# A recurrent memory layer's softmax: eight groups on one path, the last four on ScalarE and GpSimd, and a filler unit in three parts

## The chip, the core and the metric

The kernel runs on one core of one Trainium2 chip. A core has five engines that run side by side and meet through semaphores: TensorE (PE in the profile; its weight loads are listed as PEld), VectorE (DVE), ScalarE (ACT), GpSimd (POOL) and SyncE (SP), whose queue issues most DMAs here. The metric is the device time of one execution, in microseconds; lower is better. The kernel before takes 2867.46 us (median of 3 runs, 2866.17 to 2868.26).

## What is computed

Four layers run one after the other, A, B, A, B, each added to the residual stream x (2048 tokens of width 640), each behind a LayerNorm. The change lies in layer B, a transformer with recurrent memory:

```python
def _B_ref(x, mem0, Wq, Wk, Wv, Wo, seg_len):   # H = 32 heads of Dh = 128, M = 8, seg_len = 32
    mask = (idx[:, None] < M) | (idx[:, None] >= idx[None, :])
    mem = mem0
    for s in range(n_seg):                       # 64 segments
        xs = x[:, s * seg_len:(s + 1) * seg_len, :].copy()
        h = jnp.concatenate([mem, xs], axis=1)   # 8 memory rows, then 32 tokens
        q, k, v = (jnp.einsum('btd,dhe->bhte', h, W) for W in (Wq, Wk, Wv))
        scores = jnp.where(mask[None, None], jnp.einsum('bhqe,bhke->bhqk', q, k) * scale, -1e9)
        p = _softmax(scores, axis=-1)
        o = jnp.einsum('bhqk,bhke->bhqe', p, v)
        o = jnp.einsum('bhte,hed->btd', o, Wo)
        mem = o[:, :M, :].copy()                 # the next segment starts from these rows
        outs.append(o[:, M:, :])
```

The memory rows of a segment are the output of the segment before, so the 64 steps of a layer B can't overlap freely: the projections of step s+1 need the output rows of step s.

## The kernel before

`layer_B` (line 543 on) runs its 64 steps in one loop. All instructions are issued through a recording layer (`_OrdEng`, line 91 on; that is why almost all of B's instructions carry line 105 in the profile, and are told apart by their tiles). It chains the instructions of TensorE, ScalarE, VectorE and GpSimd in the order in which the program writes them. So the order in the source is the order in each of these engines' queues, and an instruction that waits holds all that stand behind it on its engine. SyncE's queue isn't chained: a scheduler places the DMAs in it.

A step s works on 32 columns: eight rows of memory for the next segment and 24 tokens of this one. In order:

- *Projections.* `thin_mm` multiplies the 32 columns by four blocks of the weights (b_Ka, b_Qa, b_Kb, b_Qb: 20 matmuls each). The results are copied to SBUF (b_kq), transposed (b_TPak, b_TPaq, b_TPbk, b_TPbq), and scattered to b_KT and b_QT.
- *Scores.* There are 12 groups of 128 rows by 40 keys. Groups 0 to 7 lie in one PSUM tile (b_SP0), groups 8 to 11 in a second (b_SP1); `GR` holds these bounds.
- *Softmax.* `soft_max` takes the negated row maximum of a tile (VectorE), `soft_sub` adds it to the scores in PSUM (VectorE), `soft_exp` takes the exponential into E_ (ScalarE), `soft_sum` sums the rows (VectorE). One reciprocal makes rs for all 12 groups, and `soft_p` multiplies: columns 32 to 40 into Pm, columns 0 to 32 into Px (VectorE).
- *Behind it on GpSimd*, `tails_copy(s + 1)` copies the scores' operands of the next segment's last eight tokens from b_tl to b_QZ and b_KT. b_tl is one buffer, loaded by SyncE (`tails_load`).
- *V.* b_Va and b_Vb, 20 matmuls each, need no softmax; ScalarE copies them to b_Vth.
- *Tail unit.* In the first 55 steps of a layer (s up to 54), `tail_unit` computes eight heads (five matmuls each, b_tail) for the last eight tokens of later segments. The kernel before puts five heads ahead of the transposes of P and three behind them; `tail_evac` then copies the result (b_tu, ScalarE) and stores it. The last nine steps of a layer have no such unit.
- *Transposes of P.* `p_transp(0)` transposes groups 4 to 7 and 0 to 3, `p_transp(1)` groups 8 to 11 and again 0 to 3, first from Pm, then from Px, into b_PTP. They are copied to SBUF: b_PTa by ScalarE in two halves, b_PTb by VectorE.
- *PV and the output.* `pv(0)` reads b_PTa, `pv(1)` b_PTb; both write four tiles b_OTP, which VectorE and ScalarE copy to b_OTsb. Matmuls with b_wo follow (b_OPSd for the rows of four segments together, b_OPS), a copy of the result (b_msb), and the transposes of the memory rows (b_MT), which VectorE writes into the next columns (b_HX). There the next step starts.

Tiles that change hands every step are few: E_, Px, Pm, b_PTa and b_PTb have one buffer each, negmax, ssum and rs two. The tiles of PSUM from `ps_tile` share five buffers, b_tail has one of its own.

Of the kernel before, what the change touches and what calls it, by code (L numbers as in the profile page):

```python
# [18 lines left out]
F32 = mybir.dt.float32  # L19
BF16 = mybir.dt.bfloat16  # L20
ACT = mybir.ActivationFunctionType
ALU = mybir.AluOpType
# [15 lines left out]
def alloc_consts(tc, ctx):  # L38
    cp = ctx.enter_context(tc.tile_pool(name="consts", bufs=1))
    C = Consts()  # L40
    C.pool = cp
    C.identb = cp.tile([128, 128], BF16, name="c_identb")
    C.mhalf = cp.tile([128, 1], F32, name="c_mhalf")
    C.negu = cp.tile([128, 2, 128], BF16, name="c_negu")
    C.krow = cp.tile([128, 1], F32, name="c_krow")
    C.bdmask = cp.tile([128, 128], F32, name="c_bd")
    W = AWeights()
    W.g = cp.tile([128, 32], F32, name="a_g")
    W.omg = cp.tile([128, 32], F32, name="a_omg")
    return C, W  # L50


def build_consts(nc, tc, C):
    with ExitStack() as tctx:
        tp_ = tctx.enter_context(tc.tile_pool(name="consts_tmp", bufs=1))
        ones = tp_.tile([128, 128], F32, name="c_ones")
        nc.vector.memset(ones[:], 1.0)
        identf = tp_.tile([128, 128], F32, name="c_identf")
        nc.gpsimd.affine_select(out=identf[:], in_=ones[:], pattern=[[-1, 128]], compare_op=ALU.is_equal,
                                fill=0.0, base=0, channel_multiplier=1)  # L60
        nc.vector.tensor_copy(C.identb[:], identf[:])
        nc.vector.memset(C.mhalf[:], -0.5)
        negs = tp_.tile([128, 128], F32, name="c_negs")
        nc.vector.memset(negs[:], -1e9)
        neguf = tp_.tile([128, 128], F32, name="c_neguf")
        nc.gpsimd.affine_select(out=neguf[:], in_=negs[:], pattern=[[1, 128]], compare_op=ALU.is_gt,
                                fill=0.0, base=0, channel_multiplier=-1)
        for i in range(2):
            nc.vector.tensor_copy(C.negu[:, i, :], neguf[:])
        krows = tp_.tile([128, 4, 2], F32, name="c_krows")  # L70
        nc.vector.tensor_copy(krows[:], identf[:].rearrange("p (j s) -> p j s", s=32)[:, :, 20:22])
        nc.vector.tensor_reduce(out=C.krow[:], in_=krows[:].rearrange("p j s -> p (j s)"), axis=AX.X, op=ALU.add)
        nc.vector.memset(C.bdmask[:], 0.0)
        for j in range(4):
            nc.vector.memset(C.bdmask[32 * j:32 * j + 32, 32 * j:32 * j + 32], 1.0)
# [467 lines left out]
def layer_B(nc, tc, C, W, x_src, xb_src, x_dst, mem0, B_Wv, B_Wo, nsteps=64, out_bf16=False, tag=""):  # L543
    SCB = 1.0 / math.sqrt(128.0)
    nc_raw = nc
    nc = _OrdNC(tc, nc_raw, engines=ORDER_ENGINES)
# [4 lines left out]
    with ExitStack() as ctx:  # L551
# [21 lines left out]
        def ps_tile(shape, dtype, name):  # L573
            return pp.tile(shape, dtype, name=name, tag="ps")


        Px = st.tile([128, 12, 32], BF16, name="b_Px")
        Pm = st.tile([128, 12, 32], BF16, name="b_Pm")
# [39 lines left out]
        def evac(eng, dst, src, scale=None):  # L618
            if eng == "act":
                if scale is None:  # L620
                    nc.scalar.copy(dst, src)
                else:
                    nc.scalar.activation(out=dst, in_=src, func=ACT.Copy, scale=scale)
            else:
                if scale is None:
                    nc.vector.tensor_copy(dst, src)
                else:
                    nc.vector.tensor_scalar(out=dst, in0=src, scalar1=scale, scalar2=None, op0=ALU.mult)
# [72 lines left out]
        def tail_unit(T, k, i0, i1, shared=False):  # L701
            proj, hg = divmod(k, 4)
            Wt = W.wk if proj else W.wq
            if i0 == 0:
                if shared:
                    tail_ps[0] = ps_tile([128, 8, 64], F32, "b_tail")
                else:
                    tail_ps[0] = po.tile([128, 8, 64], F32, name="b_tail", tag="tail")
            ps = tail_ps[0]
            for i in range(i0, i1):  # L710
                h = 8 * hg + i
                for c in range(NCH):
                    nc.tensor.matmul(ps[:, i, :], lhsT=Wt[:, c, 128 * h:128 * h + 128], rhs=TX[T][:, c, :, :].rearrange("p s t -> p (s t)"),
                                     start=(c == 0), stop=(c == NCH - 1))
# [139 lines left out]
        for s in range(nsteps):  # L854
# [3 lines left out]
            unit = None  # L858
            if (s + 1) // 8 + 1 < NT:
                unit = ((s + 1) // 8 + 1, (s + 1) % 8)  # L860
# [15 lines left out]
            GR = ((0, 8), (8, 12))  # L876

            def mask_mm(a):
                g0, g1 = GR[a]
                SP = ps_tile([128, g1 - g0, 40], F32, f"b_SP{a}")  # L880
                nc.tensor.matmul(SP[:].rearrange("p g k -> p (g k)"), lhsT=C.identb[:], rhs=mask12[:, g0:g1, :].rearrange("p g k -> p (g k)"),
                                 start=True, stop=False, skip_group_check=True)
                return SP
# [18 lines left out]
            negmax = sm.tile([128, 12], F32, name="b_negmax", tag="negmax")  # L902
            ssum = sm.tile([128, 12], F32, name="b_ssum", tag="ssum")
            rs = sm.tile([128, 12], F32, name="b_rs", tag="rs")
            E_ = wk.tile([128, 12, 40], BF16, name="b_E", tag="E0")

            def soft_max(a, SP):
                nc.vector.tensor_reduce(out=negmax[:, slice(*GR[a])], in_=SP[:], axis=AX.X, op=ALU.max, negate=True)

            def soft_sub(a, SP):  # L910
                n_ = GR[a][1] - GR[a][0]
                nc.vector.tensor_tensor(out=SP[:], in0=SP[:], in1=negmax[:, slice(*GR[a])].unsqueeze(2).to_broadcast([128, n_, 40]), op=ALU.add)

            def soft_exp(a, SP):
                nc.scalar.activation(out=E_[:, slice(*GR[a]), :], in_=SP[:], func=ACT.Exp)

            def soft_sum(a):
                nc.vector.tensor_reduce(out=ssum[:, slice(*GR[a])], in_=E_[:, slice(*GR[a]), :], axis=AX.X, op=ALU.add)

            def soft_p(P_, k0, k1, g0, g1):  # L920
                nc.vector.tensor_tensor(out=P_[:, g0:g1, 0:k1 - k0], in0=E_[:, g0:g1, k0:k1],
                                        in1=rs[:, g0:g1].unsqueeze(2).to_broadcast([128, g1 - g0, k1 - k0]), op=ALU.mult)

            def p_transp(b):
                ptp = ps_tile([128, 2, 4, 40], F32, "b_PTP")
                sel = C.identb[:, 64 * b:64 * b + 64].rearrange("p (i c) -> p i c", c=32)[:, :, 0:16]
                for part, P_ in ((1, Pm), (0, Px)):
                    nc.tensor.matmul(ptp[:, part, :, 8:40], lhsT=P_[:, 4 + 4 * b:8 + 4 * b, :].rearrange("p g k -> p (g k)"), rhs=C.identb[:],
                                     start=True, stop=True, skip_group_check=True)
                    nc.tensor.matmul(ptp[:, part, :, 0:8], lhsT=P_[:, 0:4, :].rearrange("p g k -> p (g k)"), rhs=sel,  # L930
                                     start=True, stop=True, skip_group_check=True)
                return ptp
# [33 lines left out]
            SPb = mask_mm(1)  # L966
            scores((SPa, SPb))
            soft_max(0, SPa)
            soft_max(1, SPb)
            soft_sub(0, SPa)  # L970
            soft_exp(0, SPa)
            soft_sub(1, SPb)
            soft_exp(1, SPb)
            soft_sum(0)
            soft_sum(1)
            nc.vector.reciprocal(out=rs[:], in_=ssum[:])
            soft_p(Pm, 32, 40, 0, 12)
            soft_p(Px, 0, 32, 0, 8)
            soft_p(Px, 0, 32, 8, 12)
            if not last:  # L980
                tails_copy(s + 1, tl)
            VH[s] = w2.tile([128, 2, 512], BF16, name="b_Vth", tag="Vth")
# [3 lines left out]
            evac("act", VH[s][:, 1, :], Vb[:])  # L986

            if unit:
                tail_unit(unit[0], unit[1], 0, 5)
            if ln_ready:  # L990
                ln_spread(ln_ready.pop(0))
            ptpa = p_transp(0)
            PTa = wk.tile([128, 2, 4, 40], BF16, name="b_PTa", tag="PTa")
            for hf in range(2):
                evac("act", PTa[:, :, 2 * hf:2 * hf + 2, :], ptpa[:, :, 2 * hf:2 * hf + 2, :])
            ptpb = p_transp(1)
            PTb = wk.tile([128, 2, 4, 40], BF16, name="b_PTb", tag="PTb")
            evac("dve", PTb[:], ptpb[:])
            if unit:
                tail_unit(unit[0], unit[1], 5, 8)  # L1000
                tail_evac(unit[0], unit[1], "act")
            ots = [ps_tile([128, 2, 4, 40], F32, "b_OTP") for _ in range(4)]
            pv(0, PTa, ots)
# [144 lines left out]
```

## Time and profile before

| | |
|---|---|
| median of three runs | 2867.46 us (2866.17 to 2868.26) |
| the profiled execution | 2871.54 us |
| its span, first to last instruction | 2869.8 us |
| mean granted clock of TensorE | 0.975 |
| one step of B with a tail unit, from one b_Ka to the next (most of them) | 14.97 to 15.4 us |
| one step of B without a tail unit | 14.97 us, or about 16.7 us |
| b_ssum, eight groups / four groups (VectorE) | 486 / 309 ns |
| b_SP minus its maximum, eight / four (VectorE) | 490 / 323 ns |
| b_E, eight / four (ScalarE) | 437 / 298 ns |
| b_Px, eight / four (VectorE) | 418 / 284 ns |
| b_PTa, one of two halves (ScalarE) / b_PTb (VectorE) | 300 / 492 ns |

The profile lists each instruction with its engine, its start and its end. A group's row reads: line, engine, operation, output tile from input tile, shapes and types, count, then busy time, mean duration, and the idle time of the engine ahead of it with what ended most of it. A row "x2" in a timeline joins two neighbours of one kind, and its length runs from the start of the first to the end of the last. The chain of waits follows the work back from the last instruction, at each step to what released it. A row of windows gives, for a stretch, the busy time of each engine and the clock that TensorE was granted. TensorE's matmuls are pipelined, and their ends are modelled.

### The profile page before, as it was taken

The numbers are of one execution on the slowest core, as the hardware profiler recorded it, in microseconds if no ns is written. First come the engines' busy times: TensorE is split into PE (matmuls) and PEld (weight loads), VectorE is DVE, ScalarE is ACT, GpSimd is POOL, SyncE is SP. The second block draws the span as 40 slices with busy tenths as digits, with TensorE's granted clock in tenths as the row PEclk, the third lists the DMA queues.
The fourth block names the chain that finished last, engine by engine and source line by source line (L and its number), as shares of the span: only waits on it lengthen the run. The fifth ranks groups of instructions, "written<-read, shape, count | busy, mean of one in ns | idle before, by whom it ended". The sixth has DMA issues, their size and how long they took to land.

```text
span 2869.8 us, 145239 instructions
## 1 busy us (share of the span) xinstructions
PE 2671.2 (93%) x64776; PEld 1669.4 (58%) x64776; DVE 1646.2 (57%) x4428; ACT 1555.7 (54%) x3390; POOL 633.2 (22%) x1506
## 2 busy tenths in 40 slices
PE   5899998999999999999969999889999999999988
PEld 2455555666666666665535555556666666666655
DVE  5778854555555555544468878545555555555544
ACT  3777863545445455544438777544455455445533
POOL 3456551100000000000025666400000000010000
PEclk8999999999999999999989999999999999999999
DMA  5110144222221122111130111621111111111110
GB/s 212 53 43 28 33 142 118 44 43 43 44 43 42 42 46 43 40 40 29 23 120 20 57 47 35 198 71 40 42 39 38 43 41 41 42 39 38 38 22 19
DMA packets 322947, 156.40 MB, mean 54 GB/s; under 512 B 245776, under 2 KB 311056, under 8 KB 319248
## 3 DMA queue, kind: packets, MB, share of 16 engines
q1 hardware_dynamic: 320880, 136.63, 18.8%
q8 instruction: 506, 8.29, 1.2%
q10 hardware_dynamic: 1440, 10.49, 1.0%
q14 instruction: 121, 0.99, 0.1%
HBM read 95.65 MB, written 51.38 MB: 51 GB/s over the span
## 4 chain that ended last, share of the span: by engine, by line
PE 61%; DVE 13%; ACT 4%; DMA 3%; issue 2%; POOL 1%; SPq 0%; ACTq 0%; DVEq 0%; POOLq 0%
PE b_OPS L105 11%; PE b_Ka L105 6%; PE b_Qb L105 5%; PE b_Kb L105 5%; PE b_Qa L105 5%; PE b_SP L105 4%; PE b_OTP L105 3%; PE b_OPSd L105 3%; DVE b_ssum L105 3%; PE b_tail L105 2%; PE b_vtail L105 2%; DVE b_negmax L105 2%; PE b_PTP L105 2%; DVE b_SP L105 2%; ACT b_E L105 2%
## 5 line engine op out<-in xcount | busy, mean ns | idle before, releaser
L105 PEld LDWEIGHTS <-b_HX 128*32 128x32 bf16 x15360 | 412.1, 97 | 374.1 <-issue 16.5
L375 DVE TENSOR_REDUCE a_nm<-a_S 128x2 f32<-128x1024 f32 (+3 forms) x512 | 403.5, 811 | 92.3 <-PE a_T L407 70.8
L410 ACT ACTIVATE a_PT<-a_T 128x1024 bf16<-128x1024 f32 (+1 forms) x384 | 341.0, 892 | 51.9 <-PE a_T L407 46.7
L105 POOL COPY b_OTdef<-b_OTsb 128x256 bf16<-128x256 bf16 x128 | 51.2, 400 | 1360.0 <-DVE b_OTsb L105 1288.6
L105 PE MATMUL b_OPS<-b_wo,b_OTsb 128*32 128x320 bf16 x8192 | 327.0, 311 | 12.7 <-issue 7.6
L105 PEld LDWEIGHTS <-b_OTsb 128*32 128x32 bf16 x8192 | 217.0, 100 | 104.2 <-DVE b_OTsb L105 28.1
L412 POOL TENSOR_SCALAR_AFFINE_SELECT a_PT<-a_PT 128x256 bf16<-128x256 bf16 (+1 forms) x384 | 197.3, 516 | 235.6 <-ACT a_PT L410 234.4
L105 ACT CAST b_msb<-b_OPS 128x128 bf16<-128x128 f32 x252 | 61.5, 295 | 294.2 <-PE b_OPS L105 294.2
L105 DVE CAST b_HX<-b_MT 128x16 bf16<-128x16 f32 x248 | 44.2, 178 | 268.8 <-PE b_MT L105 257.5
L105 ACT CAST b_kq<-b_Kb 128x512 bf16<-128x512 f32 x128 | 74.9, 585 | 201.4 <-PE b_Kb L105 201.4
L105 DVE TENSOR_SCALAR b_kq<-b_Qa 128x512 bf16<-128x512 f32 x128 | 88.5, 692 | 157.3 <-PE b_Qa L105 157.2
L105 DVE CAST b_OTsb<-b_OTP 128x160 bf16<-128x160 f32 (+1 forms) x384 | 122.0, 373 | 90.5 <-PE b_OTP L105 90.4
L105 PE MATMUL b_Ka<-b_wk,b_HX 128*32 128x512 bf16 x2520 | 159.2, 381 | 6.0 <-DVE b_HX L105 0.3
L105 PE MATMUL b_Va<-b_wv,b_HX 128*32 128x512 bf16 x2520 | 161.0, 380 | 0.0
L105 PE MATMUL b_Vb<-b_wv,b_HX 128*32 128x512 bf16 x2520 | 160.3, 379 | 0.0
L407 PE MATMUL a_T<-a_q,a_kT 32*128 32x512 bf16 (+3 forms) x1024 | 139.5, 306 | 21.2 <-DVE a_nm L375 14.6
L105 DVE COPY b_KT<-b_TPak 128x128 bf16<-128x128 bf16 x128 | 28.7, 224 | 227.2 <-PE b_TPak L105 227.2
L105 PE MATMUL b_Qb<-b_wq,b_HX 128*32 128x512 bf16 x2520 | 157.9, 379 | 0.0
L105 PE MATMUL b_Qa<-b_wq,b_HX 128*32 128x512 bf16 x2520 | 157.8, 379 | 0.0
L105 PE MATMUL b_Kb<-b_wk,b_HX 128*32 128x512 bf16 x2520 | 157.8, 379 | 0.0
L105 PEld LDWEIGHTS <-b_kq 128*128 128x128 bf16 x2080 | 116.9, 98 | 69.9 <-ACT b_kq L105 55.6
L105 ACT CAST b_kq<-b_Ka 128x512 bf16<-128x512 f32 x128 | 74.9, 585 | 147.0 <-PE b_Ka L105 147.0
(196 smaller groups left out, 5586.7 us busy)
## 6 DMA issues: line engine op xcount, KB each, us to landing
b_QKd<-b_tu SPq DMA_DIRECT2D x128, 128.0 KB
b_tl<-b_QKd SPq DMA_DIRECT2D x128, 128.0 KB
b_wv<-in_B_Wv_dram SPq DMA_DIRECT2D x10, 1024.0 KB
b_wo<-in_B_Wo_dram SPq DMA_DIRECT2D x16, 640.0 KB
b_VTd<-b_vt SPq DMA_DIRECT2D x256, 32.0 KB
b_Vth<-b_VTd SPq DMA_DIRECT2D x512, 16.0 KB
b_XO<-xres SPq DMA_DIRECT2D x256, 30.0 KB
b_wk<-in_B_Wk_dram ACTq DMA_DIRECT2D x5, 1024.0 KB
```

The costliest lines, as they stand in the source:

```text
L105: r = f(*a, **k)
L375: nc.vector.tensor_reduce(out=nm[:, qc, 2 * pr:2 * pr + 2], in_=X[:, :, o:o + w_], axis=AX.X, op=ALU.max, negate=True)
L407: nc.tensor.matmul(Y[:, e, o:o + w_], lhsT=kT[rows, 128 * kc:128 * kc + 128], rhs=q2[rows, 128 * kc:512], start=True, stop=True, tile_posi ...
L410: nc.scalar.activation(out=PT[:, :, b:b + width], in_=Y[:, :, 0:width], func=ACT.Exp, scale=SC)
L412: nc.gpsimd.affine_select(out=dv, in_=dv, pattern=[[0, 2], [0, diag], [1, 128]], compare_op=ALU.is_ge, fill=0.0, base=0, channel_multiplie ...
```

## The change

- The softmax of groups 0 to 7 runs to its end ahead of the rest: the maximum of the last four groups is taken after the subtraction of the first eight, and the sum, the reciprocal and the products of the first eight follow without the others.
- The last four groups aren't subtracted on VectorE. ScalarE takes their exponential one group at a time, in four instructions, with the negated maximum as a bias per row and the row sum as a second output (`soft_exp_rows`).
- Their reciprocal is taken on GpSimd as a power of minus one (`C.mone` is a new constant of -1), and GpSimd also makes their Pm and Px, ahead of `tails_copy`.
- `p_transp(0)` reads only what VectorE made; `p_transp(1)` waits for GpSimd.
- b_PTa is copied whole, by VectorE; b_PTb by ScalarE.
- The tail unit stands in three parts: four heads ahead of `p_transp(0)`, two between it and `p_transp(1)`, two behind.

In the built program SyncE's queue differs too: the load of b_tl for a later segment stands ahead of the store of b_tu and the loads of b_Vth, where it stood behind them.

```diff
@@ constants @@
+    C.mone = cp.tile([128, 1], F32, name="c_mone")
...
+        nc.vector.memset(C.mone[:], -1.0)
@@ layer_B @@
+            def soft_exp_rows(a, SP):
+                g0, g1 = GR[a]
+                for g in range(g0, g1):
+                    nc.scalar.activation(out=E_[:, g, :], in_=SP[:, g - g0, :], func=ACT.Exp, bias=negmax[:, g:g + 1], scale=1.0,
+                                         accum_out=ssum[:, g:g + 1])
...
-            def soft_p(P_, k0, k1, g0, g1):
-                nc.vector.tensor_tensor(out=P_[:, g0:g1, 0:k1 - k0], in0=E_[:, g0:g1, k0:k1],
-                                        in1=rs[:, g0:g1].unsqueeze(2).to_broadcast([128, g1 - g0, k1 - k0]), op=ALU.mult)
+            def soft_p(eng, P_, k0, k1, g0, g1):
+                eng.tensor_tensor(out=P_[:, g0:g1, 0:k1 - k0], in0=E_[:, g0:g1, k0:k1],
+                                  in1=rs[:, g0:g1].unsqueeze(2).to_broadcast([128, g1 - g0, k1 - k0]), op=ALU.mult)
...
             soft_max(0, SPa)
-            soft_max(1, SPb)
             soft_sub(0, SPa)
             soft_exp(0, SPa)
-            soft_sub(1, SPb)
-            soft_exp(1, SPb)
+            soft_max(1, SPb)
+            soft_exp_rows(1, SPb)
             soft_sum(0)
-            soft_sum(1)
-            nc.vector.reciprocal(out=rs[:], in_=ssum[:])
-            soft_p(Pm, 32, 40, 0, 12)
-            soft_p(Px, 0, 32, 0, 8)
-            soft_p(Px, 0, 32, 8, 12)
+            nc.vector.reciprocal(out=rs[:, 0:8], in_=ssum[:, 0:8])
+            soft_p(nc.vector, Pm, 32, 40, 0, 8)
+            soft_p(nc.vector, Px, 0, 32, 0, 8)
+            nc.gpsimd.tensor_tensor(out=rs[:, 8:12], in0=ssum[:, 8:12], in1=C.mone[:, 0:1].to_broadcast([128, 4]), op=ALU.pow)
+            soft_p(nc.gpsimd, Pm, 32, 40, 8, 12)
+            soft_p(nc.gpsimd, Px, 0, 32, 8, 12)
...
             if unit:
-                tail_unit(unit[0], unit[1], 0, 5)
+                tail_unit(unit[0], unit[1], 0, 4)
...
-            for hf in range(2):
-                evac("act", PTa[:, :, 2 * hf:2 * hf + 2, :], ptpa[:, :, 2 * hf:2 * hf + 2, :])
+            evac("dve", PTa[:], ptpa[:])
+            if unit:
+                tail_unit(unit[0], unit[1], 4, 6)
             ptpb = p_transp(1)
...
-            evac("dve", PTb[:], ptpb[:])
+            evac("act", PTb[:], ptpb[:])
             if unit:
-                tail_unit(unit[0], unit[1], 5, 8)
+                tail_unit(unit[0], unit[1], 6, 8)
                 tail_evac(unit[0], unit[1], "act")
```

## The prediction

> **What bounds the kernel now.** I read the page first, its chain of waits, then that chain in order of time for one step of B, then the windows that show the clock.
>
> ```profile
> PE 2671.2 (93%) x64776; PEld 1669.4 (58%) x64776; DVE 1646.2 (57%) x4428; ACT 1555.7 (54%) x3390; POOL 633.2 (22%) x1506
> PE 61%; DVE 13%; ACT 4%; DMA 3%; issue 2%; POOL 1%; SPq 0%; ACTq 0%; DVEq 0%; POOLq 0%
> ...
> 1154.52 0.55 DVE b_negmax L105 x2
> ...
> 1155.16 0.50 DVE b_SP L105
> ...
> 1155.74 0.45 ACT b_E L105
> ...
> 1156.21 0.72 DVE b_ssum L105 x2
> ...
> 1156.96 0.24 DVE b_rs L105
> ...
> 1157.22 0.26 DVE b_Pm L105
> 1157.48 0.34 DVE b_Px L105
> ...
> 1157.87 0.45 PE b_PTP L105 x6
> 1158.32 0.45 PE b_tail L105 x15
> ```
>
> A busy share of 93% would say that TensorE sets the time. The chain says otherwise: in every step it leaves TensorE for the softmax and returns at the transposes of P, although V and 25 tail matmuls run meanwhile. I call 1154.52 zero of this step. The transposes of the eight groups' Px start at 3.35, those of the last four at 3.45 (Pm) and 3.56 (Px), and the part of PV that reads PTb starts at 4.42 (timeline of TensorE). From there all is one chain to the next step, so what moves 4.42 moves the step, and 128 steps run one after the other. 110 of them hold a tail unit (s up to 54, in two layers); 18 don't.
>
> ```profile
> 1308.70:1312.10 3.40, 2.26 (x92) 1.68 (x88) 2.14 (x9) 1.51 (x5) 0.00 (x0) 1.00 0.07 15
> 1312.10:1315.50 3.40, 3.40 (x56) 2.00 (x56) 1.55 (x5) 0.48 (x2) 1.21 (x4) 0.51 0.10 25
> ...
> 1325.80:1329.20 3.40, 2.33 (x100) 1.80 (x104) 2.32 (x9) 1.69 (x6) 0.00 (x0) 1.00 0.00 0
> 1329.20:1332.60 3.40, 3.40 (x60) 2.10 (x52) 0.27 (x1) 0.09 (x1) 1.22 (x4) 0.50 0.12 28
> 1342.90:1346.30 3.40, 2.80 (x112) 2.17 (x116) 2.21 (x7) 1.33 (x5) 0.06 (x1) 1.00 0.00 0
> 1346.30:1349.70 3.40, 2.92 (x84) 1.71 (x80) 0.99 (x4) 0.49 (x2) 1.16 (x4) 1.00 0.08 20
> ```
>
> The columns are stretch, length, busy time of PE, PEld, DVE, ACT, POOL, then granted clock. These are steps without a tail unit. Where PE was idle 1.14 or 1.07 us of 3.4, the next 3.4 us ran at half clock; after 0.60 idle they didn't. A halved step takes 16.75 us (K projections at 1317.11 and 1333.86), the next, unhalved one 14.97: 1.78 us. 12 of the 18 were halved, none of the 110.
>
> **The change, part by part.** DVE first. It loses the second subtraction (323 ns), the second sum (309), the second Px (284) and a third of Pm. Eight groups in the new order: reduce 0 to 0.49; subtraction 0.52 to 1.01; exp on ScalarE from 1.10 for 0.44, to 1.54; the second reduce lies under it (0.93 to 1.24); sum 1.57 to 2.05; reciprocal to 2.31; Pm 2.35 to 2.60; Px, which overlaps Pm by 0.08, 2.52 to 2.94. Durations are the groups' means, gaps those of the chain. Before, Px was ready at 3.31 (1157.83), so the first half comes 0.37 earlier. TensorE is there in time: 20 tail matmuls at 0.035 (15 took 1158.17 to 1158.70) from 2.13 end at 2.83, the first Px transposes start at 3.00, end their issue at 3.10, and 10 tail matmuls more bring TensorE to the last four groups at 3.45.
>
> Those go ScalarE, GpSimd, TensorE. The rows:
>
> ```profile
> L297 ACT ACTIVATE a_kT<-a_KP,c_krow 128x512 bf16<-128x512 f32 x64 | 44.0, 687 | 27.3 <-PE a_KP L295 27.0
> L105 ACT ACTIVATE b_E<-b_SP 128x160 bf16<-128x160 f32 x128 | 38.2, 298 | 0.0
> L105 POOL TENSOR_TENSOR b_ln_rstd<-b_ln_rstd,c_mhalf 128x1 f32<-128x1 f32 x32 | 17.5, 548 | 370.4 <-DVE b_ln_rstd L105 355.5 <-DMA b_Vth<-b_VTd 14.9
> L380 POOL TENSOR_TENSOR a_NM<-a_nm,a_NM 128x16 bf16<-128x16 f32 x64 | 17.2, 268 | 0.7
> 1566.61 1.09 POOL L86 TENSOR_TENSOR a_ln_rstd<-a_ln_rstd,c_mhalf 128x1 f32<-128x1 f32 x1
> 1566.62 0.68 DVE L286 SCALAR_TENSOR_TENSOR a_phiq<-a_EQ,a_rq 128x512 bf16<-128x512 bf16 x1
> ```
>
> *Four rows of exp with bias and sum.* exp costs 298 ns for 160 columns and 437 for 320, so 40 cost 194; a column operand adds 102 (687 against 585 for the same shape without), neighbours overlap 0.10. First row at 1.44, the end A at the least 1.44 + 0.296 + 3 x 0.196 = 2.32. No row shows the summing output. Its bounds: nothing, or one smallest ScalarE instruction without overlap (229 ns, 128x32) per row, A = 2.32 + 4 x 0.23 = 3.24. I take the middle, 2.8, since a read-out of one column should cost less than 32.
>
> *pow of four columns.* pow of one column is 548 ns, a plain two-input op of 16 columns 268. Bounds: 0.55, if further columns are as cheap as plain ones, and 0.55 + 3 x 0.28 = 1.39. I take 0.85, nearer to the row of the same operation.
>
> *Pm and Px on GpSimd.* 16 columns 268, 128 columns 469, so 32 cost about 0.29; with a gap of 0.08 after pow, which it reads (as L446 behind L445, 3.5 us in 48), and an overlap of 0.06 (b_OTdef 1162.27 for 0.40, the next copy at 1162.61), 0.08 + 0.29 + 0.47 - 0.06 = 0.78. Starting pow after ScalarE is 0.07 (the mask op at L412 after L410), waking TensorE 0.05.
>
> So the last transposes start at R = A + 0.07 + pow + 0.78 + 0.05: **4.55** (2.8, 0.85), from 3.77 (2.32, 0.55) to 5.53 (3.24, 1.39). Below nothing the sum can't go: TensorE is there at 3.45 in any case.
>
> The last lines shown speak against the low end. pow took 1.09 instead of 0.55 beside a DVE op of two SBUF inputs that ran 0.68; it ended 0.40 after that op. For A under 2.8 the new pow lies beside DVE's Pm and Px (to 2.94), and would end at 3.34 at the earliest: R = 4.17. [...]
>
> *What is late next.* PTb's eviction begins 0.34 after the transposes start (1157.87 to 1158.21), takes 0.43 on ScalarE, and TensorE answers in 0.05. So PV's second part starts at R + 0.82 and not at 4.42: R - 3.60 = **0.95 a step**, bounds 0.17 and 1.93, and 128 x 0.95 = 122 us. On ScalarE, V's evictions move behind the rows (end A + 0.97 = 3.8, before PTb needs it at 4.9); PTa goes to DVE, 3.34 to 3.83, under tail matmuls; the tail's eviction follows PTb and ends about when PV does, as now. If that cover goes it adds 0.1. GpSimd's three tail copies (0.3, 0.3, 0.4) now stand behind Px, and the load of b_tl, which waits for them, stands in SP's queue ahead of the stores of b_tu and the loads of b_Vth: at R + 1 = 5.5 against 4.94 for b_tu now (1159.46). Those loads are wanted a step later, 10 us off: nothing. The LayerNorm pow and OTdef follow on GpSimd at about 7: nothing.
>
> *The clock.* TensorE now stands from 3.45 to R, 1.10 us in a unit step, on the edge of the 1.07 that halved it. A free window of 3.41 holds 1.07 of it in (3.41 + 1.10 - 2.14)/3.41 = 0.69 of positions; half of the steps will fall below the edge, so I charge a third: 110 x 0.33 x 1.78 = 65 us. The steps without a unit wait longer: the other 6 are halved too, 11 us.
>
> Sum: 122 + 65 + 11 = 198 us. The profiled execution took 2871.5 (span 2869.8, 1.7 around it), 4.1 over the median of 2867.5, so **3065**. [...]
>
> **The rivals.**
> *GpSimd quick (chance 0.23).* Rows and pow near the low ends: R 3.77 to 4.17, 0.17 to 0.57 a step. TensorE waits at most 0.72, under the edge, so no clock. 22 to 73 us and 11: 2900 to 2951. For it: pow's 548 ns may be mostly its start. Against: it takes both ends at once.
> *The clock in most steps (0.26).* R from 4.8: waits of 1.35 to 2.08, 1.2 to 1.93 a step, halved in 0.77 to 0.98 of unit steps: 154 + 151 + 11 to 247 + 192 + 11: 3184 to 3318. For it: pow costs 548 ns for one column already, and nothing fills the wait. Against: it needs both unknowns in their upper parts.
> *The gain is kept, faster (0.09).* The last four groups ready before TensorE, R at most 3.5 (A + pow under 2.6, 0.27 below the two low ends). Unit steps then gain 0.1, because two tail heads still stand ahead: 11 us. The 18 others gain up to 0.4, 7 us, and lose the idle time that halves the clock, up to 12 x 1.78 = 21: 2830 to 2850.
> *Even (0.04).* R about 3.6: the lost and won tenths cancel.
>
> **How the numbers follow.** Forecast 0.38 (2960 to 3180). About 0.2%, 6 us, can be told from no change. Faster 0.09, same 0.04, slower 0.87. The range runs from 2890, which leaves out the last two rivals, to 3290, which cuts the top of the clock's: 0.19 left out.
>
> **What would show it.** Right: Px's first transposes at 3.0; TensorE idle about 1 us ahead of the second b_PTP, ended by POOL; b_rs on POOL near 0.85; halved windows inside unit steps. Wrong: the second pair started by 3.6, rows that end by 2.0, or a pow under 0.4 us.

## The result, and the profile after

| | before | after |
|---|---|---|
| median | 2867.07 us (4 runs, 2866.17 to 2868.26) | 2986.39 us (4 runs, 2984.89 to 2993.48) |
| profiled execution / its span | 2871.54 / 2869.8 us | 2985.53 / 2983.8 us |
| mean granted clock | 0.975 | 0.968 |
| most common step with a tail unit | 14.97 us | 15.91 us |
| mean of the 110 steps with a unit | 15.24 us | 16.12 us |
| mean of the steps without a unit (16, the last of each layer left out) | 16.16 us | 17.21 us |

The changed kernel is slower: ratio 1.0415 [1.0391, 1.0438], 119 us. The forecast was 3065, and the time lies inside the range given with it.

First the page's busy line, then groups of the costliest instructions (busy, mean ns of one, idle of the engine ahead of it and what ended that):

```profile
PE 2704.6 (91%) x64776; PEld 1664.7 (56%) x64776; DVE 1566.2 (52%) x4045; ACT 1656.0 (56%) x4158; POOL 841.0 (28%) x1890
...
L107 POOL TENSOR_TENSOR b_rs<-b_ssum,c_mone 128x4 f32<-128x4 f32 x128 | 132.4, 1034 | 1457.0 <-ACT b_E L107 1457.0
L107 ACT ACTIVATE b_E<-b_SP,b_negmax 128x40 bf16<-128x40 f32 x512 | 143.0, 299 | 0.0
L107 ACT ACTIVATION_READ_ACCUMULATOR b_E<-b_SP,b_negmax 128x1 f32 x512 | 108.9, 213 | 0.0
L107 POOL TENSOR_TENSOR b_Px<-b_E,b_rs 128x128 bf16<-128x128 bf16 x128 | 51.3, 401 | 0.0
L107 POOL TENSOR_TENSOR b_Pm<-b_E,b_rs 128x32 bf16<-128x32 bf16 x128 | 30.8, 241 | 10.0
L107 PE MATMUL b_PTP<-c_identb,b_Pm 128*128 128x128 bf16 x256 | 57.8, 226 | 95.7 <-POOL b_Pm L107 86.2 <-DVE b_Pm L107 9.4
```

DVE lost 80 us and TensorE's busy time hardly moved. What is new stands in the last line: ahead of the transposes of Pm TensorE now waits 86.2 us in all for GpSimd's b_Pm; before, it waited 16.5 us there, for DVE:

```profile
L105 PE MATMUL b_PTP<-c_identb,b_Pm 128*128 128x128 bf16 x256 | 56.9, 222 | 16.9 <-DVE b_Pm L105 16.5
```

The chain of waits is of little use in this profile (it books 12.91 us near the end, nearly a whole step, as "issue"), so I read one step of the most common kind by engine. These timelines (start, length, engine, instruction, in brackets the idle time ahead of it and what ended it) are DVE's, ScalarE's, GpSimd's and TensorE's, of one step with a tail unit; the first line is the zero of the prediction, the first maximum.

```profile
1146.51 0.49 DVE L107 TENSOR_REDUCE b_negmax<-b_SP 128x8 f32<-128x320 f32 x1 [0.36 <-PE b_SP L107]
...
1149.09 0.42 DVE L107 TENSOR_TENSOR b_Px<-b_E,b_rs 128x256 bf16<-128x256 bf16 x1
```

```profile
1147.72 0.44 ACT L107 ACTIVATE b_E<-b_SP 128x320 bf16<-128x320 f32 x1 [0.74 <-PE b_Va L107]
1148.06 0.29 ACT L107 ACTIVATE b_E<-b_SP,b_negmax 128x40 bf16<-128x40 f32 x1
...
1149.04 0.22 ACT L107 ACTIVATION_READ_ACCUMULATOR b_E<-b_SP,b_negmax 128x1 f32 x1
...
1151.47 0.43 ACT L107 CAST b_PTb<-b_PTP 128x320 bf16<-128x320 f32 x1 [1.24 <-PE b_PTP L107]
```

```profile
1149.34 1.04 POOL L107 TENSOR_TENSOR b_rs<-b_ssum,c_mone 128x4 f32<-128x4 f32 x1 [11.29 <-ACT b_E L107]
1150.45 0.24 POOL L107 TENSOR_TENSOR b_Pm<-b_E,b_rs 128x32 bf16<-128x32 bf16 x1
1150.65 0.40 POOL L107 TENSOR_TENSOR b_Px<-b_E,b_rs 128x128 bf16<-128x128 bf16 x1
```

```profile
1149.57 0.24 PE L107 MATMUL b_PTP<-c_identb,b_Px 128*128 128x128 bf16 x2
1149.66 0.45 PE L107 MATMUL b_tail<-b_TX,b_wq 128*128 128x64 bf16 x10
1150.75 0.24 PE L107 MATMUL b_PTP<-c_identb,b_Pm 128*128 128x128 bf16 x2 [0.64 <-POOL b_Pm L107]
1151.11 0.24 PE L107 MATMUL b_PTP<-c_identb,b_Px 128*128 128x128 bf16 x2
...
1151.94 0.38 PE L107 MATMUL b_OTP<-b_PTb,b_Vth 32*128 32x40 bf16 x32
```

The eight groups' Px starts at 2.58 and its transposes at 3.06, ahead of where they stood before (3.35). ScalarE ends the four rows at 2.75. Then one engine waits for the next without a break: pow to 3.87, Pm to 4.18, Px to 4.54, the transposes of Px at 4.60, PTb from 4.96 to 5.39, PV's second part at 5.43. It stood at 4.42 before; the zero itself now lies 0.03 earlier in the step.

### The profile page after: what moved, and what is told of

Read it like the earlier page. It is cut to its first block, busy times and chain, and to the rows that moved or that the text cites. A ratio compares the mean times of both kernels' runs of the same rounds, so it can differ in the third digit from the quotient of the medians.

```text
span 2983.8 us, 145547 instructions
## 1 busy us (share of the span) xinstructions
PE 2704.6 (91%) x64776; PEld 1664.7 (56%) x64776; DVE 1566.2 (52%) x4045; ACT 1656.0 (56%) x4158; POOL 841.0 (28%) x1890
## 3 DMA queue, kind: packets, MB, share of 16 engines
q14 instruction: 123, 1.01, 0.1%
## 5 line engine op out<-in xcount | busy, mean ns | idle before, releaser
L107 POOL TENSOR_TENSOR b_rs<-b_ssum,c_mone 128x4 f32<-128x4 f32 x128 | 132.4, 1034 | 1457.0 <-ACT b_E L107 1457.0
L107 DVE TENSOR_SCALAR b_kq<-b_Qa 128x512 bf16<-128x512 f32 x128 | 88.6, 692 | 157.9 <-PE b_Qa L107 157.9
L107 PE MATMUL b_PTP<-c_identb,b_Pm 128*128 128x128 bf16 (+1 forms) x512 | 61.8, 202 | 95.7 <-POOL b_Pm L107 86.2
```

The source lines that it names most:

```text
L107: r = f(*a, **k)
```

## The experiments

All of them change a few lines of the kernel before or of the changed one. Ratios are against runs of the kernel before on the same chip. "Step" is the most common step with a tail unit (14.97 us before, 15.91 after).

### Which engine costs it: e1_recip_vector and e2_all_vector

The first gives the reciprocal of the last four groups to DVE and leaves Pm and Px on GpSimd; the second gives these two to DVE as well.

```diff
-            nc.gpsimd.tensor_tensor(out=rs[:, 8:12], in0=ssum[:, 8:12], in1=C.mone[:, 0:1].to_broadcast([128, 4]), op=ALU.pow)
+            nc.vector.reciprocal(out=rs[:, 8:12], in_=ssum[:, 8:12])
# e2_all_vector, in addition
-            soft_p(nc.gpsimd, Pm, 32, 40, 8, 12)
-            soft_p(nc.gpsimd, Px, 0, 32, 8, 12)
+            soft_p(nc.vector, Pm, 32, 40, 8, 12)
+            soft_p(nc.vector, Px, 0, 32, 8, 12)
```

> The changed kernel with the reciprocal of the last four groups on VectorE (behind Px of the first eight) in place of GpSimd's pow; Pm and Px of these groups stay on GpSimd. Theory (the pow's 1.03 us on GpSimd sets when the last transposes of P start): VectorE has the reciprocal at 9.5 of a step, GpSimd's Px ends at 10.2 and not at 10.83, so a step loses 0.63 us, 128 x 0.63 = 81: about 2905, and some 30 less where the last nine steps of a layer escape the half clock. Rival (the four rows on ScalarE, or GpSimd as such, or the tail unit in three parts cost the time): less than 40 us off, 2950 or more.

> The changed kernel with reciprocal, Pm and Px of the last four groups all on VectorE; only the four rows of exp stay on ScalarE. Theory: Px ends at 9.99, the last transposes start at 10.04, and PV's second part 0.82 later, at 10.86 against 10.73 before the change: still 0.13 a step slower than before, 128 x 0.13 = 17, about 2884. Rival (leaving GpSimd gives back the whole first-half gain of 0.37): 2820 to 2850. Rival (the tail parts and the swapped copies cost it): 2930 or more.

| | median | ratio | step |
|---|---|---|---|
| e1_recip_vector | 2885.23 us | 1.0065 [1.0046, 1.0083] | 15.22 us |
| e2_all_vector | 2854.24 us | 0.9959 [0.9937, 0.9981] | 14.87 us |

The first came out where its theory put it (2875 to 2905). Two edits return the whole loss. Of the 0.94 us that a step had grown, the pow holds 0.69 (15.91 to 15.22) and the two products on GpSimd 0.35 (15.22 to 14.87). What is left of the change takes 0.10 away. It is won behind the softmax and not in it: the last transposes of P start 9.86 after the start of the step both in the kernel before and in e2_all_vector, and the first copies of PV's output at 11.30 and 11.20. The second expectation missed on the fast side: this version is a little faster than the kernel before.

### What is left of the change: e3_tail_and_copies and e4_max_later

Two parts alone, put into the kernel before. First the tail unit in three parts with the two copies of P exchanged:

```diff
-                tail_unit(unit[0], unit[1], 0, 5)
+                tail_unit(unit[0], unit[1], 0, 4)
...
-            for hf in range(2):
-                evac("act", PTa[:, :, 2 * hf:2 * hf + 2, :], ptpa[:, :, 2 * hf:2 * hf + 2, :])
+            evac("dve", PTa[:], ptpa[:])
+            if unit:
+                tail_unit(unit[0], unit[1], 4, 6)
...
-            evac("dve", PTb[:], ptpb[:])
+            evac("act", PTb[:], ptpb[:])
             if unit:
-                tail_unit(unit[0], unit[1], 5, 8)
+                tail_unit(unit[0], unit[1], 6, 8)
```

> The kernel before with only the tail unit in three parts (4, 2, 2 heads), PTa copied whole by VectorE and PTb by ScalarE; the softmax as before. Theory: the two heads between the transposes (0.35 us) now delay the second transposes, whose P is ready by then, and PTb's copy follows them: PV's second part at 11.03 and not 10.73, 0.30 in each of 110 steps with a unit, 33 us: about 2900. Rival (the parts are free, since the order of filler work doesn't matter to TensorE): within 6 us of the kernel before.

Measured: 2877.53 us, ratio 1.0046 [1.0028, 1.0065], step 15.12. Right in sign, about half in size (0.15 for 0.30 in the step, 13 us for 33). With the old softmax all of P is ready together, and two tail heads between the transposes hold up the second ones: those of Px start at 10.14 of the step, not at 9.86. They are not the whole cost: in steps without a unit, where no head stands there, the common step is 15.04 against 14.97, so the exchanged copies alone cost 0.07.

Then the second maximum behind the first eight groups' subtraction:

```diff
             soft_max(0, SPa)
-            soft_max(1, SPb)
             soft_sub(0, SPa)
             soft_exp(0, SPa)
+            soft_max(1, SPb)
             soft_sub(1, SPb)
```

> The kernel before with one line moved: the maximum of the last four groups behind the subtraction and exp of the first eight. Theory (the softmax is on the chain in every step): exp of the eight groups starts 0.27 earlier, the sums start when VectorE is done with the second subtraction, 0.12 earlier than before, so 128 x 0.12 = 15 us: about 2852, and up to 20 less where the last nine steps of a layer escape the half clock. Rival (TensorE's queue sets the time while V and the tail run): within 6 us of the kernel before.

Measured: 2878.84 us, ratio 1.0056 [1.0033, 1.0079], step 15.07: the wrong sign. DVE's timeline of one step shows why; first of the kernel before, then of this one:

```profile
1108.88 0.72 DVE L105 TENSOR_REDUCE b_negmax<-b_SP 128x8 f32<-128x320 f32 x2 [0.38 <-PE b_SP L105]
1109.51 0.72 DVE L105 TENSOR_TENSOR b_SP<-b_SP,b_negmax 128x320 f32<-128x320 f32 x2
1110.57 0.71 DVE L105 TENSOR_REDUCE b_ssum<-b_E 128x8 f32<-128x320 bf16 x2 [0.33 <-ACT b_E L105]
```

```profile
1113.16 0.49 DVE L105 TENSOR_REDUCE b_negmax<-b_SP 128x8 f32<-128x320 f32 x1 [0.40 <-PE b_SP L105]
1113.76 0.50 DVE L105 TENSOR_TENSOR b_SP<-b_SP,b_negmax 128x320 f32<-128x320 f32 x1
1114.17 0.32 DVE L105 TENSOR_REDUCE b_negmax<-b_SP 128x4 f32<-128x160 f32 x1
1114.59 0.33 DVE L105 TENSOR_TENSOR b_SP<-b_SP,b_negmax 128x160 f32<-128x160 f32 x1
1114.83 0.84 DVE L105 TENSOR_REDUCE b_ssum<-b_E 128x8 f32<-128x320 bf16 x2
```

Before, two maxima and two subtractions stand as independent neighbours: each second one starts before the one ahead of it has ended (two maxima of 0.49 and 0.32 take 0.72 together), and the four end at 1.35. In the new order each subtraction stands right behind the maximum that it reads and starts 0.10 to 0.11 (0.42 less 0.32, 0.60 less 0.49) after its end, and the four end at 1.76. The first subtraction starts only 0.03 sooner for it (0.60 against 0.63). So the last four groups' exponential and sum come later, and the two sums end 2.51 after the first maximum's start, not 2.40: the 0.10 of the step. Two dependent pairs in a row lose more than the earlier start wins. The change has the first of these pairs too.

### How much hangs on pow, and on the clock: e5_pow_twice

A second pow of the same four columns, into a tile that nothing reads:

```diff
+            nc.gpsimd.tensor_tensor(out=rs2[:], in0=ssum[:, 8:12], in1=C.mone[:, 0:1].to_broadcast([128, 4]), op=ALU.pow)
             nc.gpsimd.tensor_tensor(out=rs[:, 8:12], in0=ssum[:, 8:12], in1=C.mone[:, 0:1].to_broadcast([128, 4]), op=ALU.pow)
```

> The changed kernel with GpSimd's pow made twice (the first into a tile that nothing reads). Theory (pow lies on the chain, and the half clock follows idle time of TensorE over about 1 us in 3.4): every step is 1.03 longer, 128 x 1.03 = 132, and TensorE's idle time in a unit step goes from 0.83 to 1.86, so most of the 110 unit steps are halved too, up to 110 x 1.78 = 196: 3150 to 3310, with halved windows in unit steps. Rival (unit steps aren't halved, because tail matmuls stand on both sides of the wait): 3118, granted clock as in the changed kernel.

Measured: 3137.51 us, ratio 1.0973 [1.0948, 1.0998], step 16.88. The step grew by 0.97 and the second pow took 1.00: pow stands on the chain from end to end. The clock did not follow the theory. 18 of the 110 unit steps were halved, neither most of them nor none, and the time lies between the two forecasts, 3118 and 3150. A window of a step that was not halved, and the one behind it (stretch, length, busy time and count of PE, PEld, DVE, ACT, POOL, then granted clock):

```profile
638.80:642.20 3.40, 1.81 (x46) 1.13 (x35) 1.70 (x5) 1.99 (x10) 2.21 (x4) 1.00 0.00 0
642.20:645.60 3.40, 3.20 (x130) 2.41 (x134) 1.59 (x5) 1.68 (x4) 1.20 (x5) 1.00 0.32 69
```

TensorE was idle for 1.59 of 3.4 us and kept the whole clock. (In the trace of before all 49 changes of the clock lie within 0.01 us of one grid of 3.41 us, in that of after all 73; these windows are cut on such a grid.)

### Which part stands in the way: e6_tail_4_4_0

The last two tail heads go ahead of the second transposes, where TensorE waits:

```diff
-                tail_unit(unit[0], unit[1], 4, 6)
+                tail_unit(unit[0], unit[1], 4, 8)
             ptpb = p_transp(1)
...
-                tail_unit(unit[0], unit[1], 6, 8)
```

> The changed kernel with the tail unit's last two heads moved ahead of the second transposes, where TensorE waits 0.75 us in a unit step. Theory (behind the wait the copy of PTb is late next, not TensorE's own work): PV's first part starts earlier, its second part still 0.82 after the last transposes start, so the step stays 15.91 and the time within 10 us of the changed kernel's, 2986. Rival (TensorE's work behind the wait sets the rest of the step): 0.35 less in 110 steps, 38 us, 2948.

Measured: 2985.23 us, ratio 1.0429 [1.0413, 1.0444], step 15.90. Work moved into TensorE's wait bought nothing, because behind the transposes the copy of PTb on ScalarE is next and TensorE would wait there anyway: PV's first part starts at 11.05 of the step and not at 11.36, but its second at 11.71 as without the edit, when that copy (to 11.65) has ended.

### When the clock falls: e7_px_first and e12_tail_behind

In the changed kernel the transposes of Pm split TensorE's wait into 0.64 and 0.12. The first experiment puts Px ahead of Pm in the second transposes, which makes one piece of it; the second moves the whole tail unit behind the second transposes, so that TensorE has nothing to do meanwhile.

```diff
-                for part, P_ in ((1, Pm), (0, Px)):
+                for part, P_ in (((1, Pm), (0, Px)) if b == 0 else ((0, Px), (1, Pm))):
# e12_tail_behind, alone
-            if unit:
-                tail_unit(unit[0], unit[1], 0, 4)
...
-            if unit:
-                tail_unit(unit[0], unit[1], 4, 6)
...
-                tail_unit(unit[0], unit[1], 6, 8)
+                tail_unit(unit[0], unit[1], 0, 8)
```

> The changed kernel with the two last transposes of P exchanged for the last four groups: Px first, then Pm. TensorE then waits for GpSimd's last product in one piece (9.78 to 10.88, 1.10 us) and not in two (0.64 and 0.11, with the Pm transposes between them). Theory (idle time over about 1 us in a 3.4 us window halves the clock): up to 0.69 of the 110 unit steps are halved, 110 x 0.69 x 1.78 = 135, and the second transposes follow 0.10 later, 11 to 13 us: 3050 to 3130. Rival (the clock doesn't go by idle time in this place): 0.10 a step alone, about 3000, no halved windows in unit steps.

> The changed kernel with the whole tail unit behind the second transposes: in a unit step nothing is left between V and the transposes, and TensorE is idle about 1.65 us of 3.4, as in steps without a unit; but behind the wait stand 40 full-array matmuls and not PV. In both theories PV comes 0.97 later, 110 x 0.97 = 107 us. Theory 1 (idle time over about 1 us alone halves the clock): most unit steps are halved as well, 60 to 190 us more, 3150 to 3290. Theory 2 (PV's small matmuls in the window count as idle too, dense matmuls in it do not, which is why unit steps with 1.6 us idle stayed at full clock): few unit steps are halved, 3080 to 3120.

| | median | ratio | step | unit steps halved |
|---|---|---|---|---|
| after | 2986.39 us | 1.0415 [1.0391, 1.0438] | 15.91 us | 5 of 110 |
| e7_px_first | 2996.64 us | 1.0466 [1.0451, 1.0482] | 15.98 us | 6 of 110 |
| e5_pow_twice | 3137.51 us | 1.0973 [1.0948, 1.0998] | 16.88 us | 18 of 110 |
| e12_tail_behind | 3091.13 us | 1.0785 [1.0755, 1.0815] | 16.70 us | 17 of 110 |

The windows, first of e7_px_first, then two pairs of e12_tail_behind:

```profile
592.80:596.20 3.40, 2.33 (x96) 1.96 (x97) 1.26 (x4) 2.08 (x8) 2.44 (x6) 1.00 0.00 0
596.20:599.60 3.40, 3.40 (x128) 2.56 (x127) 1.83 (x5) 1.24 (x4) 0.40 (x1) 1.00 0.44 92
```

```profile
605.60:609.00 3.40, 1.86 (x30) 0.84 (x22) 2.10 (x7) 2.50 (x11) 1.46 (x3) 1.00 0.08 18
609.00:612.40 3.40, 3.29 (x144) 2.72 (x146) 0.95 (x3) 1.78 (x4) 0.99 (x4) 1.00 0.20 49
...
622.70:626.10 3.40, 1.76 (x27) 0.68 (x20) 1.84 (x6) 2.50 (x11) 1.70 (x4) 1.00 0.06 14
626.10:629.50 3.40, 3.40 (x114) 3.15 (x118) 0.22 (x1) 1.23 (x3) 0.74 (x3) 0.50 0.12 39
```

1.07 us of idle time in one window, which went with a halved clock in steps without a unit, leaves the clock whole in e7_px_first (0.99 of it is the one wait for GpSimd). In e12_tail_behind 1.54 us left it whole and 1.64 us halved it. So "idle for more than 1.07 us in 3.4" is not the rule. For e7_px_first the rival was right in time (about 3000), though 6 unit steps were halved where it had none. For e12_tail_behind theory 1 falls; theory 2, that idle time alone does not decide, was right in time (3080 to 3120).

### Looking for a faster version: e8 to e11

All start from e2_all_vector, which leaves only the copies of P between the transposes and PV. e8_ptb_halves splits the copy of PTb between ScalarE and DVE, e9_pm_gpsimd gives Pm of the last four groups back to GpSimd, beside DVE's Px, and e10_both_copies_vector gives all of PTb to DVE:

```diff
# e8_ptb_halves
-            evac("act", PTb[:], ptpb[:])
+            for hf, eng in ((0, "act"), (1, "dve")):
+                evac(eng, PTb[:, :, 2 * hf:2 * hf + 2, :], ptpb[:, :, 2 * hf:2 * hf + 2, :])
# e9_pm_gpsimd
-            soft_p(nc.vector, Pm, 32, 40, 8, 12)
+            soft_p(nc.gpsimd, Pm, 32, 40, 8, 12)
# e10_both_copies_vector, and e11_again
-            evac("act", PTb[:], ptpb[:])
+            evac("dve", PTb[:], ptpb[:])
```

> The kernel with everything but the four rows on VectorE (0.4% faster than the kernel before), with PTb copied in two halves, one by ScalarE and one by VectorE side by side. Theory (the copy of PTb is late next): it ends at 10.55 of a step and not at 10.72, PV's second part starts when the first has been issued, at 10.60 and not at 10.77: 0.15 x 128 = 19 us, ratio to the kernel before about 0.989. Rival (TensorE or the copies of PV's output bound this place already): no change, ratio 0.996.

> The kernel with everything but the four rows on VectorE (0.4% faster than the kernel before), with Pm of the last four groups given to GpSimd, beside VectorE's Px of the same groups. Theory (two products side by side): VectorE's Px ends 0.11 earlier, at 9.70; GpSimd's Pm runs 9.44 to 9.70; the step is 0.1 shorter, 13 us, ratio to the kernel before about 0.991. [...]

> The kernel with everything but the four rows on VectorE, with PTb copied by VectorE too, behind PTa, so that ScalarE has only the tail's copy. Theory (the copy of PTb is late next): VectorE has PTa from 9.72 to 10.21 and PTb from 10.13 to 10.62, against ScalarE's 10.30 to 10.72: PV's second part 0.10 earlier, 13 us, ratio to the kernel before about 0.991. Rival (PV's output copies and TensorE's own queue set what follows): ratio 0.996 as without it.

> The fastest version again (the four rows on ScalarE, all other softmax work and both copies of the transposed P on VectorE, tail unit in parts of 4, 2 and 2), to settle whether it is faster than the kernel before: ratio 0.9945 as measured once, and in any case under 0.998; the rival, that chips differ by as much, gives an interval that holds 1.

| | median | ratio |
|---|---|---|
| e8_ptb_halves | 2860.91 us | 0.9993 [0.9983, 1.0003] |
| e9_pm_gpsimd | 2857.70 us | 0.9978 [0.9961, 0.9995] |
| e10_both_copies_vector | 2848.47 us | 0.9945 [0.9923, 0.9968] |
| e11_again (the same kernel, more rounds) | 2850.36 us | 0.9950 [0.9933, 0.9966] |

The halves of e8_ptb_halves don't run side by side. Its timeline:

```profile
1108.50 0.29 ACT L107 CAST b_PTb<-b_PTP 128x160 bf16<-128x160 f32 x1 [0.20 <-PE b_PTP L107]
...
1108.82 0.32 DVE L107 CAST b_PTb<-b_PTP 128x160 bf16<-128x160 f32 x1 [0.32 <-ACT b_PTb L107]
```

DVE's half waits for ScalarE's, with which it shares the source and the target tile: a semaphore puts the two in order. Two halves one after the other take 0.64, a whole copy 0.43.

In e9_pm_gpsimd two products run at once, on GpSimd and on DVE:

```profile
L107 POOL TENSOR_TENSOR b_Pm<-b_E,b_rs 128x32 bf16<-128x32 bf16 x128 | 32.3, 252 | 1502.2 <-DVE b_rs L107 1269.3 <-PE b_lntps L107 232.9
...
L107 DVE TENSOR_TENSOR b_Px<-b_E,b_rs 128x128 bf16<-128x128 bf16 x128 | 37.3, 292 | 4.4
```

Alone they took 241 and 285 ns (after, and e2_all_vector), here 252 and 292. They overlap by only 0.15 us, so whether one would hold the other up in a longer overlap is not shown. GpSimd's product starts 0.17 after DVE's reciprocal, which goes with a step longer by 0.06 (14.93 against 14.87), though the two ratios' intervals overlap. The theory missed: it had the step 0.1 shorter, and its 0.991 lies outside the interval.

e10_both_copies_vector is the fastest kernel here. PTb needs no other engine to wake:

```profile
1116.52 0.48 DVE L107 CAST b_PTa<-b_PTP 128x320 bf16<-128x320 f32 x1
1116.95 0.49 DVE L107 CAST b_PTb<-b_PTP 128x320 bf16<-128x320 f32 x1
```

Its copy is longer than ScalarE's (0.49 against 0.43) but follows at once, and in the median over the unit steps PV's output is copied 0.08 earlier (11.22 after the start of the step, against 11.30). That is not shown to be worth time: in the most common step the copy starts at 11.21 against 11.20, this step is no shorter (14.88 against 14.87), the times of e10_both_copies_vector and e2_all_vector have overlapping intervals, and the theory's 0.991 lies outside the interval while the rival's 0.996 lies inside. That this version beats the kernel before, by 0.5%, two separate measurements show.

## Why the prediction was right, and where it was not

The direction and the mechanism held: the softmax of the first eight groups does end earlier, and that is worth nothing, since the last four now pass ScalarE and GpSimd in a row. By its own steps:

| step | predicted | measured |
|---|---|---|
| first Px transposes | 3.00 | 3.06 |
| A, end of the four rows | 2.8 | 2.75 |
| pow of four columns | 0.85 | 1.03 |
| Pm and Px on GpSimd, with gap and overlap | 0.78 | 0.67 |
| R, last transposes | 4.55 | 4.60 |
| growth of a unit step | 0.95 | 0.94 (most common), 0.82 (mean of those not halved) |
| clock, unit steps | 65 us | 8 us |
| sum | 198 us | 119 us |

- *The clock term failed, and it is most of the difference (57 of 79 us).* A third of the 110 unit steps was charged as halved; 5 were. These took 17.57 us in the mean, 1.52 more than the mean of the others (16.05): 5 x 1.52 = 8 us against 65. Two things were wrong in that step. TensorE's wait was taken as one piece of 1.10 us, but the transposes of Pm stand in it and the two pieces are 0.64 and 0.12; in the window of a unit step TensorE was idle for 0.83:

```profile
1149.00:1152.40 3.40, 2.57 (x112) 2.00 (x112) 1.00 (x3) 2.15 (x6) 2.45 (x6) 1.00 0.00 0
1152.40:1155.80 3.40, 3.40 (x108) 2.39 (x100) 2.59 (x8) 1.24 (x4) 0.91 (x2) 1.00 0.45 92
```

And the edge of 1.07 us was read from steps without a unit and carried to steps with one. e7_px_first made the wait 0.99 in one piece, 1.07 idle in the window, and 6 steps were halved; e5_pow_twice and e12_tail_behind show windows of unit steps that keep the clock at 1.54 to 1.59. So idle time was a poor measure; in the windows shown the work of the array, estimated at the end, goes better with the falls.

- *The unit steps' own growth was right in the common step and a little high in the mean.* 110 steps x 0.82 = 90 us, against 110 x 0.95 = 105. In the kernel before more of the unit steps are longer than the common 14.97 (their mean is 15.24), and those grew less. What they wait for was not followed up.
- *pow was mis-sized downwards and the products upwards, and the two nearly cancel.* One column costs 548 ns and four 1034, so 0.16 us for each further column: between the two bounds, 0.55 and 1.39. The products' rows were 241 and 401 ns where 290 and 470 had been read from plain copies and products of other shapes.
- *The rows on ScalarE came out as taken.* The summing output, for which no row stood, is an instruction of its own (213 ns), which overlaps both its neighbours; a row of 40 columns follows the one before it after 0.27 us.
- *The steps without a unit* grew by 1.05 in the mean: 18 x 1.05 = 19 us. The prediction had 18 x 0.95 + 11 = 28. All but one of the 16 were now halved. A window of one, and the next:

```profile
1391.40:1394.80 3.40, 1.76 (x30) 0.71 (x26) 1.74 (x5) 2.30 (x11) 1.91 (x5) 1.00 0.00 0
1394.80:1398.20 3.40, 3.19 (x106) 2.06 (x108) 0.95 (x3) 1.18 (x3) 0.94 (x3) 0.50 0.20 51
```

90 + 8 + 19 = 117 us, and the spans of the two profiled executions differ by 114.

- *What was costed at nothing was nothing.* The copies for the next segment stand behind Px on GpSimd and end 5.4 us after zero; the idle time that GpSimd's b_QZ spent on a DMA fell from 88.6 to 15.2 us.
- *The step by which the low end was lifted* (pow held up beside a DVE instruction with two SBUF inputs) was not put to the test. It was an estimate from one row. In the trace of before, the three pows of one column that a DVE instruction on a_phiq runs beside as they start took 1.09, 1.09 and 0.99 us, and each ended 0.41 to 0.42 after that instruction; two that it reached only 0.24 after their start took 0.55. Whether other operations are held up so, no run shows: the new pow overlapped DVE's Px by 0.17 us and took 1.034 us, where the second pow of e5_pow_twice, with no such neighbour, took 1.00; and the two products of e9_pm_gpsimd took 252 and 292 ns against 241 and 285 alone.

## What to carry to other kernels

A softmax split by groups gains only what its last group gains: an earlier first half is lost when the second half takes a longer way through other engines, so price the whole way of the last part, wake-ups included. Ahead of a move to GpSimd look for a row of that operation at that size, since its cost may grow with columns that are nearly free elsewhere (GpSimd's pow of one column 0.55 us, of four 1.03; DVE's reciprocal of four 0.17, of eight 0.20). A clock edge read in one kind of step is not to be carried to a kind with other matmuls in the window, unless a run has shown it there: here 1.07 us of idle time in 3.4 went with a halved clock in a step without a unit (before), and left it whole in a window of a step with one (e7_px_first).

## What the runs showed of the hardware that I had not expected

- An activation with a summed output is two entries in the trace of after: ACTIVATE of 299 ns and ACTIVATION_READ_ACCUMULATOR of 213 ns, at a pitch of 0.27 us for 128x40.
- DVE started a subtraction 0.10 to 0.11 us after the end of the maximum that it reads, with nothing between them (e4_max_later), while independent neighbours overlapped by about 0.1 (two maxima 0.09, two subtractions 0.11 in the kernel before).
- The clock: idle times of 1.07 us (without a unit, in the kernel before) and 1.64 us (e12_tail_behind) were followed by a halved clock, idle times of 1.07 (e7_px_first), 1.54 (e12_tail_behind) and 1.59 us (e5_pow_twice) were not. In the windows that kept it at 1.07, many small matmuls stood (96), in those at 1.5 few (30 to 46), and in those of the kernel before that went with a halved clock at 1.07 to 1.14 there were 92 and 100: neither the idle time nor the count of matmuls orders them.
- What goes with the falls in the windows shown is the work of the array, an estimate from the records of the traces. It takes each matmul's columns times the share of a 128*128 listing that its own listing makes up (128*32 is a quarter), spreads them over its record, and counts 0.42 ns a column (the 20 matmuls of b_Va, 512 columns at a quarter each, take 1.08 us up to the first of b_Vb). The windows with 1.01 and 1.20 us of it (the halved ones of the kernel before), 1.00 (after) and 1.14 (e12_tail_behind) were followed by a halved clock; those with 1.63 (before), 1.37 (after), 1.47 (e7_px_first), 1.32 (e12_tail_behind) and 1.32 (e5_pow_twice) were not. The 40 tail matmuls of a unit step are listed as 128*128, those of the projections as 128*32. These are nine windows, and no run was made to test it.
